# Attention beside an MLP: who copies the scores and the sums out of PSUM, and in which order

## The chip, the cores and the metric

The kernel runs on one core of a Trainium2 chip. The metric is the device time of one execution in microseconds (us), as the median of several runs. The core has five engines that run side by side and wait for each other by semaphores: TensorE (PE; its weight loads are PEld), VectorE (DVE), ScalarE (ACT), GpSimd (POOL) and SyncE (SP), which here issues the transfers (DMA). TensorE writes only to PSUM, which has eight banks of 128 x 512 fp32 elements. VectorE and ScalarE read PSUM; GpSimd does not.

## The reference

Shapes: x is 1 x 2048 x 448; 16 query heads of 28 columns share one key head and one value head; the MLP is 1792 wide. All is fp32.

```python
def _A_ref(x, wq, wk, wv, wo):
    q = (x @ wq).reshape(B, S, 16, 28).transpose(0, 2, 1, 3)
    k = x @ wk
    v = x @ wv
    p = softmax(einsum("bhqd,bkd->bhqk", q, k) * 28 ** -0.5)
    o = einsum("bhqk,bkd->bhqd", p, v)
    return o.transpose(0, 2, 1, 3).reshape(B, S, 448) @ wo

def _B_ref(x, w1, w2):
    return maximum(x @ w1, 0) @ w2

xn = layernorm(x)
return x + _A_ref(xn, wq, wk, wv, wo) + _B_ref(xn, w1, w2)
```

## The kernel before

The program has two parts. The first, up to about 338 us, normalizes and transposes x, makes queries, keys and values (kept in a scratch in DRAM) and runs the MLP into the accumulator `acc`. The second is the attention, and the change is there.

The attention runs over 16 units `u`, each of 512 queries (a block `b`) and four heads (a group `g`); `b` is the outer loop. A unit has 2048 keys, which are 16 key blocks `kb` of 128. It runs in two halves of 8 key blocks. A half has two stages, one after the other on TensorE:

- The score stage: 32 score matmuls (8 key blocks x 4 heads), each 128 keys x 512 queries into one PSUM bank (line 588). A string of letters in `HALVES` gives their order. For an "a", the bank is of the pool `psA` (four banks), and ScalarE reads it and writes the exponential to the tile `p` in SBUF (line 605). For a "d", the bank is of `psD` (three banks), and VectorE copies the raw score to `p` (line 610); ScalarE makes the exponential later, from SBUF in place, four heads at a time (line 623). "a" fills the key blocks from 0 up, "d" those from `KA` = 5 up, so that 20 scores go the first way and 12 the second.
- The PV run: for each key block, the four heads' matmuls of `p` with the values (line 477, `pv`). They are listed as eight matmul instructions a block. They add up in one bank over the unit's 16 key blocks; `vtile` has columns of ones, so that the softmax sums come out as further rows. We call what is in this bank the sums. Before, it is a pool of its own, `psO`, of one bank.

The first half's run leaves its last block (`behind`), which goes first in the second half's run; the second half's run thus has nine blocks and ends the unit. In the first half's run, at place `MPOS`, stand the maxima of the next unit (`maxima`, line 370): a few score matmuls into a "d" bank, a transpose and a reduction on VectorE, and eight small DMAs that put the negated estimates in two further rows of the next unit's query stack `qst`. The score matmul then subtracts them (114 rows: four times 28 and these two).

When a unit's last block is done, ScalarE copies the sums to `oS` (line 480), and four DMAs spread the denominators (`dens`). Later, at the letter "R" in the next unit's first half, `recips` takes the reciprocals on VectorE, writes them to DRAM and reads them back spread over the partitions (`rb`), and `normalized` multiplies and splits on GpSimd (`on`, `oH`, `oL`). The four output projections of that unit (`o_proj`, line 522: three matmuls of 448 columns into a "d" bank, added to `acc` by VectorE, line 524) come at the letters "F", two in each half, from the second half on. The very last half makes two at each "F". `finish` handles the sums of the last unit by itself.

Each engine works in the order of the program. A score matmul thus waits until the bank that it is to write has been read by the engine that had it, four "a" or three "d" uses earlier; an output projection is one of the "d" uses. `load_stack` loads the query stack of the unit after the next, between a first half's score stage and its run. The tiles `p` have ten buffers.

Of the kernel before, what the change touches and what calls it, by code (L numbers as in the profile page):

```python
# [8 lines left out]
F32 = mybir.dt.float32  # L9
# [29 lines left out]
def program(ctx: ExitStack, tc: tile.TileContext, HM, fine, x, wq, wk, wv, wo, w1, w2, out):  # L39
    nc = tc.nc  # L40
# [21 lines left out]
    WARM = 28  # L62
    KQ = 4 * DH
    NU = NQB * NHG
    NA, ND, NST = 4, 3, 3
    assert DR == 64 and KQ + 2 <= P and HG * 32 == P and NPART * FP == DFF

    cst = ctx.enter_context(tc.tile_pool(name="cst", bufs=1))
    small = ctx.enter_context(tc.tile_pool(name="small", bufs=2))
    dram = ctx.enter_context(tc.tile_pool(name="dram", bufs=1, space=DRAM))  # L70
    psA = ctx.enter_context(tc.tile_pool(name="psA", bufs=NA, space=PSUM))
    psD = ctx.enter_context(tc.tile_pool(name="psD", bufs=ND, space=PSUM))
    psO = ctx.enter_context(tc.tile_pool(name="psO", bufs=1, space=PSUM))


    acc = cst.tile([P, NT, D], F32, name="acc")
# [15 lines left out]
    gone = cst.tile([P, TPB + 3], F32, name="gone")  # L92
    nc.vector.memset(gone, 1.0)

    pw = psD.tile([P, QB], F32, name="d")
    for _ in range(WARM):
        nc.tensor.matmul(pw[:, 0:P], ident, ident, start=True, stop=True)  # L97
    kst = cst.tile([P, S], F32R, name="kst")
# [137 lines left out]
    def transposed(b, xn, chunks=range(DC + 1)):  # L236
        xs = slice(b * QB, (b + 1) * QB)
        for c in chunks:
            pt = psD.tile([P, QB], F32, name="d") if c < DC else psO.tile([P, QB], F32, name="o")
            for i in range(TPB):  # L240
                nc.tensor.transpose(pt[:, i * P : (i + 1) * P], xn[i][:, c * P : (c + 1) * P], ident)  # L241
            if c < DC:
                nc.scalar.activation(xH[:, c, xs], pt, AF.Copy)  # L243
                nc.vector.tensor_tensor(xL[:, c, xs], pt, xH[:, c, xs].bitcast(F32), op=ALU.subtract)  # L244
            else:
                tmp = small.tile([P, QB], F32R, name="tmp")
                nc.scalar.activation(xR[0:DR, xs], pt[0:DR], AF.Copy)
                nc.scalar.activation(tmp[DR:P], pt[DR:P], AF.Copy)
                nc.vector.tensor_tensor(xR[DR:P, xs], pt[DR:P], tmp[DR:P].bitcast(F32), op=ALU.subtract)  # L249
# [86 lines left out]

    def v_rows():

        pv = psD.tile([P, QB], F32, name="d")
        for kb in range(NKB):  # L340
            nc.tensor.transpose(pv[:, kb * 32 : kb * 32 + DH], vT[0][:, kb * P : (kb + 1) * P], ident[0:DH, 0:DH])
        nc.vector.tensor_copy(vtile[:, :, 0:DH], pv.rearrange("p (i d) -> p i d", d=32)[:, :, 0:DH])
        if fine is not None:
            nc.vector.tensor_reduce(
                gone[:, TPB : TPB + 1], vtile[:, :, 0:DH], axis=AX.XY, op=ALU.max, apply_absolute_value=True
            )
# [15 lines left out]
    def maxima(u):  # L362

        st = qst[u]

        def scores(kb):
            pm = psD.tile([P, QB], F32, name="d")
            for j in range(HG):
                c = slice(32 * j, 32 * j + 32)
                nc.tensor.matmul(  # L370
                    pm[c], kstF[0:KQ, kb * 32 : kb * 32 + 32], st.bitcast(F32)[0:KQ, j], start=True, stop=True
                )
            return pm

        n = QB // 32
        nm = small.tile([P, n], F32, name="nm")
        nm2 = small.tile([P, 2, n], F32R, name="nm2")
        rows = small.tile([P, 2 * n], F32, name="rows")
        sc = scores(0)
        if HM > 1:  # L380
            top = small.tile([P, QB], F32R, name="tmp").bitcast(F32)
            nc.vector.tensor_copy(top, sc)
            for kb in range(1, HM):
                nc.vector.tensor_tensor(top, top, scores(kb), op=ALU.max)
            sc = top
        mt = small.tile([P, QB], F32R, name="tmp").bitcast(F32)
        nc.vector.transpose(mt, sc)
        nc.vector.tensor_reduce(nm, mt.rearrange("p (c k) -> p c k", k=32), axis=AX.X, op=ALU.max, negate=True)
        nc.vector.tensor_copy(nm2[:, 0], nm)
        nc.vector.tensor_tensor(nm2[:, 1], nm, nm2[:, 0].bitcast(F32), op=ALU.subtract)  # L390
        nc.vector.transpose(rows, nm2.rearrange("p s n -> p (s n)").bitcast(F32))
        for j in range(HG):
            for s in range(2):
                r = KQ + s
                nc.sync.dma_start(
                    st.bitcast(F32)[r : r + 1, j].rearrange("o (c q) -> o c q", q=32),
                    rows[32 * j + s * n : 32 * j + s * n + n],
                )
# [17 lines left out]
    def mlp_down(p, b, i, between=None):  # L416
        hH, hL = hid[p, b]
        wd = parts[p][1]
        py = psO.tile([P, QB], F32, name="o") if i == 1 else psA.tile([P, QB], F32, name="a")
        n = 0  # L420
        for f in range(FC):
            for hm, wi in ((hH, 0), (hH, 1), (hL, 0)):
                nc.tensor.matmul(  # L423
                    py[:, 0:D], hm[:, f, i * P : (i + 1) * P], wd[:, wi, f, :], start=n == 0, stop=n == 3 * FC - 1
                )
                n += 1
            if between:
                between()
        t = b * TPB + i
        nc.vector.tensor_tensor(acc[:, t, :], py[:, 0:D], acc[:, t, :], op=ALU.add)  # L430
# [41 lines left out]
    def pv(u, kb, p):  # L472
        start, stop = kb == 0, kb == NKB - 1
        if start:
            o_acc[u] = psO.tile([P, QB], F32, name="o")
        for j in range(HG):
            nc.tensor.matmul(o_acc[u][32 * j : 32 * j + 32], vtile[:, kb, :], p[:, j], start=start, stop=stop)  # L477
        if stop and u < NU - 1:
            oS = opool.tile([P, QB], F32, name="oS")
            nc.scalar.activation(oS, o_acc.pop(u), AF.Copy)  # L480
            o_sb[u] = oS
            dens(u)

# [31 lines left out]
    def o_proj(u, i):  # L515

        b, g = units[u]
        oH, oL = o_hl[u]
        py = psD.tile([P, QB], F32, name="d")[:, 0:D]
        c = slice(i * P, (i + 1) * P)  # L520
        for n, (om, wm) in enumerate(((oH, woH), (oH, woL), (oL, woH))):
            nc.tensor.matmul(py, om[:, c], wm[:, g, :], start=n == 0, stop=n == 2)  # L522
        t = b * TPB + i
        nc.vector.tensor_tensor(acc[:, t, :], py, acc[:, t, :], op=ALU.add)  # L524
        if g == NHG - 1:
            nc.sync.dma_start(out[t * P : (t + 1) * P, :], acc[:, t, :])

    def finish(u):

        b, g = units[u]  # L530
        o = o_acc.pop(u)
        if fine is not None:
            nc.vector.tensor_reduce(gone[:, TPB + 1 : TPB + 2], dsum, axis=AX.X, op=ALU.add)
            nc.vector.scalar_tensor_tensor(
# [16 lines left out]
                nc.vector.tensor_reduce(gone[:, i : i + 1], dens, axis=AX.XY, op=ALU.add)  # L551
            nc.gpsimd.tensor_scalar(rb[:, i], r[:, i].to_broadcast([P, HG, 32]), 1.0, 0.0, op0=ALU.mult, op1=ALU.add)
        for i, c in enumerate(cols):
            pb = psD.tile([P, QB], F32, name="d")
            nc.tensor.transpose(pb[:, 0:P], rb[:, i].rearrange("p j c -> p (j c)"), ident)
            nc.vector.tensor_tensor(on[:, c], pb[:, 0:P], oS[:, c], op=ALU.mult)
        if fine is not None:
# [8 lines left out]
            nc.vector.tensor_tensor(acc[:, t, :], py[:, 0:D], acc[:, t, :], op=ALU.add)  # L566
            nc.sync.dma_start(out[t * P : (t + 1) * P, :], acc[:, t, :])
        if fine is not None:
            pg = psD.tile([P, QB], F32, name="d")
            nc.tensor.matmul(pg[0:1, 0:1], gone[:, TPB : TPB + 1], gone[:, TPB + 2 : TPB + 3], start=True, stop=True)  # L570
            nc.vector.tensor_scalar(fine, pg[0:1, 0:1], 1e20, None, op0=ALU.is_le)

# [6 lines left out]

    HALVES = "adaadaadFaaaddadaaaFadaadadaRdadada", "adaadaadddaaadaFaadaadFaadadaadada"
    KA, KH, MPOS = 5, NKB // 2, 3
    todo = []

    def score(u, kb, j, p, pt):
        nc.tensor.matmul(  # L588
# [1 line left out]
        )  # L590
        return p[:, j]

    for u in range(NU):
        for half, order in enumerate(HALVES):
            ps, n_a, n_d = {}, 0, KA * HG
            for k in order:
                if k in "ad":
                    n = n_a if k == "a" else n_d
                    kb, j = n // HG, n % HG
                    if j == 0:  # L600
                        ps[kb] = ppool.tile([P, HG, QB], F32, name="p")
                if k == "a":
                    pt = psA.tile([P, QB], F32, name="a")
# [1 line left out]
                    nc.scalar.activation(p, pt, AF.Exp, scale=SCALE)  # L605
                    n_a += 1
                elif k == "d":
                    pt = psD.tile([P, QB], F32, name="d")
                    p = score(u, half * KH + kb, j, ps[kb], pt)
                    nc.vector.tensor_copy(p, pt)  # L610
                    n_d += 1
                elif k == "R" and u:
                    recips(u - 1)
                    normalized(u - 1)
                    todo += [(u - 1, i) for i in range(TPB)]
                elif k == "F":
                    for _ in range(2 if half and u == NU - 1 else 1):
                        if todo:
                            o_proj(*todo.pop(0))
            if half == 0 and u:  # L620
                load_stack(u + NST - 1)
            for kb in range(KA, KH):
                nc.scalar.activation(ps[kb], ps[kb], AF.Exp, scale=SCALE)  # L623
            run = [(half * KH + kb, ps[kb]) for kb in range(KH)]
            if half:
                run.insert(0, behind)
            else:
                behind = run.pop()
            for n, (kb, p) in enumerate(run):
                if half == 0 and n == MPOS and u < NU - 1:  # L630
                    maxima(u + 1)
                pv(u, kb, p)
    assert not todo
    finish(NU - 1)


# [23 lines left out]
```

## Time and profile before

| | us |
|---|---|
| median of 3 runs | 883.08 (882.75 to 883.5) |
| the profiled execution | 882.62 |
| its span, from the first to the last instruction | 880.8 |
| TensorE busy | 871.0 (99%) |
| ScalarE busy | 562.2 (64%) |
| VectorE busy | 471.0 (53%) |
| attention, from the first score to the end of the span | 338.1 to 880.8 |

Busy shares are over the whole span; in the attention they are different, and are shown below by stage. A profile line has the source line, the engine, the operation, the tile written and the tiles read, the shape and a count; then either start and length, or total busy time, mean length in ns and idle time. A matmul's length includes its way through the array, and matmuls overlap, so that only the distance between two starts says what one costs.

### The profile page before, as it was taken

To read this page: it belongs to the slowest core of one execution; us is meant where nothing else is said; L and a number is where in the kernel's file an instruction comes from. 1 tells how busy PE (TensorE), PEld (TensorE's weight loads), DVE (VectorE), ACT (ScalarE), POOL (GpSimd) and SP (SyncE) were. 2 spreads that over 40 slices of the span, in tenths; PEclk is the share of its full clock that TensorE was granted. 3 is DMA by queue.
4 is the path that set the end of the run, shared out by engine and by line. 5 is a ranking of instruction groups with operands and counts; after the bars stand their busy time and mean duration, and the time that the engine had idled before them with its cause. 6 is when DMAs were issued, how large, how long until landed. Compare 5 with 4: busy or idle time off the path is not lost.

```text
span 880.8 us, 12946 instructions
## 1 busy us (share of the span) xinstructions
PE 871.0 (99%) x4998; PEld 573.0 (65%) x4998; DVE 471.0 (53%) x848; ACT 562.2 (64%) x871; POOL 113.3 (13%) x96
## 2 busy tenths in 40 slices
PE   9999999999999999999999999999999999999996
PEld 8788888888888886454554554554554554554562
DVE  6833344333333346474574574574574574574563
ACT  4541111111111116999999999999999999999993
POOL 3034202020202003010110110110110110110110
PEclk9999999999999999999999999999999999999998
DMA  6868050010000001020120230120230120230001
GB/s 214 293 200 167 4 132 23 23 45 1 1 1 1 0 2 38 2 56 25 33 56 21 57 77 21 36 56 20 58 77 15 42 56 17 62 77 14 2 13 46
DMA packets 37502, 45.89 MB, mean 52 GB/s; under 512 B 13640, under 2 KB 24072, under 8 KB 37264
## 3 DMA queue, kind: packets, MB, share of 16 engines
q1 hardware_dynamic: 37432, 44.98, 19.7%
q8 instruction: 41, 0.67, 0.3%
q14 instruction: 29, 0.24, 0.1%
HBM read 32.37 MB, written 12.18 MB: 51 GB/s over the span
## 4 chain that ended last, share of the span: by engine, by line
PE 98%; DVE 1%; ACT 1%; issue 0%; POOL 0%; POOLq 0%
PE o L477 25%; PE a L588 19%; PE a L187 16%; PE a L423 12%; PE d L588 10%; PE d L522 4%; PE o L423 4%; PE a L192 4%; PE d L370 2%; PE a L271 1%; PE d L97 1%; PE d L241 1%; ACT p L623 0%; PE a L565 0%; DVE qs L255 0%
## 5 line engine op out<-in xcount | busy, mean ns | idle before, releaser
L610 DVE COPY p<-d 128x512 f32<-128x512 f32 x384 | 246.1, 686 | 161.7 <-PE d L588 142.1
L605 ACT ACTIVATE p<-a 128x512 f32<-128x512 f32 x640 | 317.1, 708 | 21.7 <-PE a L588 21.7
L477 PE MATMUL o<-p,vtile 128*32 128x512 f32 x2048 | 229.5, 594 | 0.0
L588 PE MATMUL a<-qst,kst 114*128 114x512 f32 x640 | 225.4, 407 | 0.0
L410 ACT ACTIVATE hH<-a 128x512 fp32r<-128x512 f32 x56 | 33.5, 598 | 235.9 <-PE a L192 235.9
L623 ACT ACTIVATE p<-p 128x2048 f32<-128x2048 f32 x96 | 183.1, 2131 | 0.0
L588 PEld LDWEIGHTS a<-qst,kst 114*128 114x128 f32 x640 | 120.0, 187 | 77.2 <-ACT p L605 28.1
L477 PEld LDWEIGHTS o<-p,vtile 128*32 128x32 f32 x2048 | 61.6, 109 | 144.1 <-issue 128.3
L588 PE MATMUL d<-qst,kst 114*128 114x512 f32 x384 | 145.8, 400 | 0.0
L187 PE MATMUL a<-xH,w 128*128 128x512 f32 x408 | 104.8, 392 | 0.2 <-ACT xH L243 0.2
L411 DVE SCALAR_TENSOR_TENSOR hL<-a,hH 128x512 fp32r<-128x512 f32 x56 | 38.7, 692 | 118.4 <-ACT hH L410 118.4
L423 PE MATMUL a<-w,hH 128*128 128x448 f32 x336 | 95.6, 366 | 0.0
L187 PEld LDWEIGHTS a<-xH,w 128*128 128x128 f32 x408 | 76.1, 188 | 16.5 <-ACT xH L243 0.8
L588 PEld LDWEIGHTS d<-qst,kst 114*128 114x128 f32 x384 | 72.4, 188 | 12.9 <-DVE p L610 4.5
L508 POOL TENSOR_TENSOR on<-rb,oS 128x512 f32<-128x512 f32 x15 | 19.4, 1290 | 448.4 <-DMA rb<-rscr 418.0
L430 DVE TENSOR_TENSOR acc<-a,acc 128x448 f32<-128x448 f32 x84 | 52.2, 622 | 33.7 <-PE a L423 33.7
L423 PEld LDWEIGHTS a<-w,hH 128*128 128x128 f32 x336 | 63.0, 188 | 6.3
L423 PE MATMUL a<-w,hL 128*128 128x448 f32 x168 | 61.2, 364 | 0.0
L187 PE MATMUL a<-xL,w 128*128 128x512 f32 x204 | 57.7, 390 | 0.1
L187 PEld LDWEIGHTS a<-xL,w 128*128 128x128 f32 x204 | 38.3, 188 | 8.8 <-DVE xL L244 0.7
L192 PE MATMUL a<-xR,w 128*128 128x512 f32 x136 | 42.0, 390 | 0.2 <-DVE xR L249 0.2
L524 DVE TENSOR_TENSOR acc<-d,acc 128x448 f32<-128x448 f32 x60 | 37.3, 622 | 5.3 <-PE d L522 5.3
(111 smaller groups left out, 577.4 us busy)
## 6 DMA issues: line engine op xcount, KB each, us to landing
qst<-qscr SPq DMA_DIRECT2D x64, 224.0 KB
qscr<-qs SPq DMA_DIRECT2D x16, 512.0 KB
rb<-rscr SPq DMA_DIRECT2D x60, 64.0 KB
acc<-in_A_x SPq DMA_DIRECT2D x16, 224.0 KB
out<-acc SPq DMA_DIRECT2D x16, 224.0 KB
stg<-in_B_w SPq DMA_DIRECT2D x7, 448.0 KB
stg<-in_B_w SPq DMA_DIRECT2D x7, 384.0 KB
qst<-rows SPq DMA_DIRECT2D x128, 2.0 KB
```

Source lines behind the costliest of these rows:

```text
L187: nc.tensor.matmul(ps, lhs[:, wi, c, cols], xm[:, c, xs], start=n == 0, stop=False)
L192: nc.tensor.matmul(ps, lhs[:, wi, DC, cols], xR[:, xs], start=False, stop=wi == 1)
L411: nc.vector.scalar_tensor_tensor(hL[:, f], ph, 0.0, hH[:, f].bitcast(F32), op0=ALU.max, op1=ALU.subtract)
L423: nc.tensor.matmul(py[:, 0:D], hm[:, f, i * P : (i + 1) * P], wd[:, wi, f, :], start=n == 0, stop=n == 3 * FC - 1)
L430: nc.vector.tensor_tensor(acc[:, t, :], py[:, 0:D], acc[:, t, :], op=ALU.add)
L477: nc.tensor.matmul(o_acc[u][32 * j : 32 * j + 32], vtile[:, kb, :], p[:, j], start=start, stop=stop)
L522: nc.tensor.matmul(py, om[:, c], wm[:, g, :], start=n == 0, stop=n == 2)
L524: nc.vector.tensor_tensor(acc[:, t, :], py, acc[:, t, :], op=ALU.add)
L588: nc.tensor.matmul(pt, kst[0 : KQ + 2, kb * P : (kb + 1) * P], qst[u][0 : KQ + 2, j, :], start=True, stop=True)
L605: nc.scalar.activation(p, pt, AF.Exp, scale=SCALE)
L610: nc.vector.tensor_copy(p, pt)
L623: nc.scalar.activation(ps[kb], ps[kb], AF.Exp, scale=SCALE)
```

## The change

- VectorE, not ScalarE, copies the sums out of PSUM.
- A half has 19 "a" scores and 13 "d" scores (`HA` = 19). Key block 4 of a half is mixed: three heads by ScalarE, one by VectorE, with an exponential of one head later.
- `psD` now has four banks, named d0 to d3 and handed out in a ring by `d_tile`; `psO` is gone. The bank with the sums is taken out of the ring (`keep`) and comes back when the sums have been copied. The few other users of `psO` use the ring.
- Every PV run leaves its last block to the next run, over the border of units too, except at the end of the last two units. A unit's block 15 is thus the first block of the next unit's first run.
- "R" moves to near the end of the second half (`ends` does it for the units that have ended); in the last unit it stands after each half's score stage. The projections of a unit start one half later, and the last half makes three at each "F".
- The maxima move from the fourth to the second place of the first half's run.
- Both strings in `HALVES` are new.

```diff
-    NA, ND, NST = 4, 3, 3
+    NA, ND, NST = 4, 4, 3
...
-    psD = ctx.enter_context(tc.tile_pool(name="psD", bufs=ND, space=PSUM))
-    psO = ctx.enter_context(tc.tile_pool(name="psO", bufs=1, space=PSUM))
+    psD = ctx.enter_context(tc.tile_pool(name="psD", bufs=1, space=PSUM))
+    ring = [f"d{i}" for i in range(ND)]
+
+    def d_tile(keep=False):
+        name = ring.pop(0)
+        if not keep:
+            ring.append(name)
+        t = psD.tile([P, QB], F32, name=name)
+        return (t, name) if keep else t
...
     def pv(u, kb, p):
         start, stop = kb == 0, kb == NKB - 1
         if start:
-            o_acc[u] = psO.tile([P, QB], F32, name="o")
+            o_acc[u] = d_tile(keep=True)
+        o = o_acc[u][0]
         for j in range(HG):
-            nc.tensor.matmul(o_acc[u][32 * j : 32 * j + 32], vtile[:, kb, :], p[:, j], start=start, stop=stop)
+            nc.tensor.matmul(o[32 * j : 32 * j + 32], vtile[:, kb, :], p[:, j], start=start, stop=stop)
         if stop and u < NU - 1:
             oS = opool.tile([P, QB], F32, name="oS")
-            nc.scalar.activation(oS, o_acc.pop(u), AF.Copy)
+            nc.vector.tensor_copy(oS, o)
+            ring.append(o_acc.pop(u)[1])
             o_sb[u] = oS
             dens(u)
...
-    HALVES = "adaadaadFaaaddadaaaFadaadadaRdadada", "adaadaadddaaadaFaadaadFaadaadadaada"
-    KA, KH, MPOS = 5, NKB // 2, 3
-    todo = []
+    HALVES = "adadadaadaadadaFaaddadaaFadaaddaad", "adadadaadaaddaadaFadaadadaFadaaRdad"
+    HA, KH = 19, NKB // 2
+    todo, behind, ended = [], [], []
...
+    def ends():
+        for u in ended:
+            recips(u)
+            normalized(u)
+            todo.extend((u, i) for i in range(TPB))
+        ended.clear()
...
     for u in range(NU):
+        last = u == NU - 1
         for half, order in enumerate(HALVES):
-            ps, n_a, n_d = {}, 0, KA * HG
+            ps, n_a, n_d = {}, 0, HA
...
-                elif k == "R" and u:
-                    recips(u - 1)
-                    normalized(u - 1)
-                    todo += [(u - 1, i) for i in range(TPB)]
-                elif k == "F":
-                    for _ in range(2 if half and u == NU - 1 else 1):
+                elif k == "R":
+                    ends()
+                else:
+                    for _ in range(3 if last and half else 1):
                         if todo:
                             o_proj(*todo.pop(0))
+            if last:
+                ends()
             if half == 0 and u:
                 load_stack(u + NST - 1)
-            for kb in range(KA, KH):
-                nc.scalar.activation(ps[kb], ps[kb], AF.Exp, scale=SCALE)
-            run = [(half * KH + kb, ps[kb]) for kb in range(KH)]
-            if half:
-                run.insert(0, behind)
-            else:
-                behind = run.pop()
-            for n, (kb, p) in enumerate(run):
-                if half == 0 and n == MPOS and u < NU - 1:
+            for kb in range(HA // HG, KH):
+                h = slice(max(HA - kb * HG, 0), HG)
+                nc.scalar.activation(ps[kb][:, h], ps[kb][:, h], AF.Exp, scale=SCALE)
+            run = behind + [(u, half * KH + kb, ps[kb]) for kb in range(KH)]
+            behind = [] if half and u >= NU - 2 else [run.pop()]
+            for n, (v, kb, p) in enumerate(run):
+                if half == 0 and n == 1 and not last:
                     maxima(u + 1)
-                pv(u, kb, p)
-    assert not todo
+                pv(v, kb, p)
+                if kb == NKB - 1 and not (last and half):
+                    ended.append(v)
+    assert not todo and not behind
     finish(NU - 1)
```

More of the change, by code (lines that the diff above doesn't have):

```diff
@@ L93, in program @@
     nc.vector.memset(gone, 1.0)
-    pw = psD.tile([P, QB], F32, name="d")
+    pw = d_tile()
     for _ in range(WARM):
@@ L238, in transposed @@
         for c in chunks:
-            pt = psD.tile([P, QB], F32, name="d") if c < DC else psO.tile([P, QB], F32, name="o")
+            pt = d_tile()
             for i in range(TPB):
@@ L337, in v_rows @@
     def v_rows():
-        pv = psD.tile([P, QB], F32, name="d")
+        pv = d_tile()
         for kb in range(NKB):
@@ L366, in scores @@
         def scores(kb):
-            pm = psD.tile([P, QB], F32, name="d")
+            pm = d_tile()
             for j in range(HG):
@@ L418, in mlp_down @@
         wd = parts[p][1]
-        py = psO.tile([P, QB], F32, name="o") if i == 1 else psA.tile([P, QB], F32, name="a")
+        py = d_tile() if i == 1 else psA.tile([P, QB], F32, name="a")
         n = 0
@@ L518, in o_proj @@
         oH, oL = o_hl[u]
-        py = psD.tile([P, QB], F32, name="d")[:, 0:D]
+        py = d_tile()[:, 0:D]
         c = slice(i * P, (i + 1) * P)
@@ L530, in finish @@
         b, g = units[u]
-        o = o_acc.pop(u)
+        o = o_acc.pop(u)[0]
         if fine is not None:
@@ L553, in finish @@
         for i, c in enumerate(cols):
-            pb = psD.tile([P, QB], F32, name="d")
+            pb = d_tile()
             nc.tensor.transpose(pb[:, 0:P], rb[:, i].rearrange("p j c -> p (j c)"), ident)
@@ L568, in finish @@
         if fine is not None:
-            pg = psD.tile([P, QB], F32, name="d")
+            pg = d_tile()
             nc.tensor.matmul(pg[0:1, 0:1], gone[:, TPB : TPB + 1], gone[:, TPB + 2 : TPB + 3], start=True, stop=True)
             nc.vector.tensor_scalar(fine, pg[0:1, 0:1], 1e20, None, op0=ALU.is_le)
-    HALVES = "adaadaadFaaaddadaaaFadaadadaRdadada", "adaadaadddaaadaFaadaadFaadadaadada"
-    KA, KH, MPOS = 5, NKB // 2, 3
-    todo = []
+    HALVES = "adadaadadaadadaFaaddadaaFadaaddaad", "adadadaadaaddaadaFadaadadaFaadaRdad"
+    HA, KH = 19, NKB // 2
+    todo, behind, ended = [], [], []
     def score(u, kb, j, p, pt):
@@ L599, in program @@
                     kb, j = n // HG, n % HG
-                    if j == 0:
+                    if kb not in ps:
                         ps[kb] = ppool.tile([P, HG, QB], F32, name="p")
@@ L607, in program @@
                 elif k == "d":
-                    pt = psD.tile([P, QB], F32, name="d")
+                    pt = d_tile()
                     p = score(u, half * KH + kb, j, ps[kb], pt)
```

## The prediction

> **What bounds the kernel now.** I read the page's busy shares and chain first, to see which engine to follow, then busy time by stage, then the timeline of TensorE, ScalarE and VectorE over one attention unit.
>
> ```profile
> PE 871.0 (99%) x4998; PEld 573.0 (65%) x4998; DVE 471.0 (53%) x848; ACT 562.2 (64%) x871; POOL 113.3 (13%) x96
> ...
> PE 98%; DVE 1%; ACT 1%; issue 0%; POOL 0%; POOLq 0%
> ```
>
> Both point at TensorE, but a matmul that waits for a PSUM bank also counts as busy. So the question is how far apart the matmuls start. The stages, in the view of busy time by stretch (length first, then each engine):
>
> ```profile
> 338.12:347.04 8.92, 8.92 (x34) 5.33 (x32) 7.23 (x12) 8.43 (x18) 2.44 (x2) 1.00 0.41 92
> 354.04:363.02 8.98, 8.98 (x36) 5.39 (x32) 7.19 (x12) 8.44 (x18) 0.00 (x0) 1.00 0.03 4
> 370.91:380.04 9.13, 9.13 (x36) 5.38 (x32) 6.71 (x13) 8.92 (x19) 0.00 (x0) 1.00 0.01 1
> ...
> 602.59:611.77 9.18, 9.18 (x43) 6.76 (x39) 7.65 (x15) 8.92 (x19) 0.00 (x0) 1.00 0.01 1
> 611.77:618.78 7.01, 7.01 (x66) 1.97 (x65) 3.20 (x8) 6.84 (x7) 0.70 (x1) 1.00 0.53 129
> 618.78:627.80 9.02, 9.02 (x42) 6.76 (x38) 7.97 (x13) 8.43 (x18) 2.51 (x3) 1.00 0.32 86
> 627.80:635.69 7.89, 7.89 (x73) 2.14 (x73) 0.78 (x2) 6.84 (x7) 0.00 (x0) 1.00 0.00 0
> ...
> 849.70:859.92 10.22, 10.22 (x49) 8.08 (x45) 9.15 (x15) 9.39 (x19) 1.44 (x2) 1.00 0.01 2
> 403.96:834.36 430.40, 430.40 (x2761) 229.66 (x2757) 259.87 (x455) 403.43 (x611) 41.80 (x39) 1.00 0.18 42
> ```
>
> The last row is 13 units: 33.11 us each. One unit is two score stages (9.18 and 9.02) and two PV runs (7.01: seven key blocks and the maxima; 7.89: nine blocks). The first three rows are the halves without output projections, 849.70 the last half, with four. The granted clock is 1.00 throughout. Now TensorE inside one unit:
>
> ```profile
> 606.79 1.12 PE L588 MATMUL a<-qst,kst 114*128 114x512 f32 x3
> 607.75 0.36 PE L522 MATMUL d<-woH,oH 128*128 128x448 f32 x1
> ...
> 608.36 0.40 PE L588 MATMUL a<-qst,kst 114*128 114x512 f32 x1
> ...
> 609.31 0.40 PE L588 MATMUL d<-qst,kst 114*128 114x512 f32 x1
> ...
> 610.93 0.42 PE L588 MATMUL a<-qst,kst 114*128 114x512 f32 x1
> ...
> 618.78 0.50 PE L588 MATMUL a<-qst,kst 114*128 114x512 f32 x1
> 619.11 0.39 PE L588 MATMUL d<-qst,kst 114*128 114x512 f32 x1
> ...
> 620.51 0.98 PE L588 MATMUL d<-qst,kst 114*128 114x512 f32 x3
> 621.32 0.85 PE L588 MATMUL a<-qst,kst 114*128 114x512 f32 x3
> ...
> 627.46 0.42 PE L588 MATMUL a<-qst,kst 114*128 114x512 f32 x1
> 627.80 7.96 PE L477 MATMUL o<-p,vtile 128*32 128x512 f32 x72
> ```
>
> From 609.31 to 610.93 lie seven scores: 0.231 each (0.232 below, with the small slips). One output projection of three matmuls takes 608.36 - 607.75 = 0.61. The first score of a stage takes 0.33, thus 0.10 extra, and the step into the PV run 0.34, 0.11 extra. A half without a wait is then 32 x 0.232 + 2 x 0.61 + 0.21 = 8.85. It takes 9.18 and 9.02, and the rows show where: three scores from 606.79 take 0.96, not 0.70 (0.26 lost); three from 620.51 take 0.81 (0.11 lost). Without these both halves are 8.91 to 8.92. The PV runs have nothing to give: 0.877 a block in 7.89, without a gap.
>
> The other two engines:
>
> ```profile
> 602.85 0.60 ACT L480 ACTIVATE oS<-o 128x512 f32<-128x512 f32 x1 [1.31 <-issue]
> 603.34 9.90 ACT L605 ACTIVATE p<-a 128x512 f32<-128x512 f32 x20
> 612.87 5.74 ACT L623 ACTIVATE p<-p 128x2048 f32<-128x2048 f32 x3
> 619.37 9.91 ACT L605 ACTIVATE p<-a 128x512 f32<-128x512 f32 x20 [0.76 <-PE a L588]
> 628.92 5.72 ACT L623 ACTIVATE p<-p 128x2048 f32<-128x2048 f32 x3
> 619.61 3.81 DVE L610 COPY p<-d 128x512 f32<-128x512 f32 x6 [2.03 <-PE d L588]
> 626.09 2.48 DVE L610 COPY p<-d 128x512 f32<-128x512 f32 x4
> L605 ACT ACTIVATE p<-a 128x512 f32<-128x512 f32 x640 | 317.1, 708 | 21.7 <-PE a L588 21.7
> L610 DVE COPY p<-d 128x512 f32<-128x512 f32 x384 | 246.1, 686 | 161.7 <-PE d L588 142.1
> ```
>
> ScalarE starts an exponential every (628.92 - 619.37) / 20 = 0.4775 us, each 0.71 long, the first 0.59 after the stage begins (619.37 - 618.78), and in a unit's first half 0.75 after, since the copy of the sums is in front. A copy train on VectorE has a step of (2.48 - 0.69) / 3 = 0.60, the first 0.83 after the stage begins. With four "a" banks the 12th "a" score of the first half must wait for the 8th exponential: 603.34 + 7 x 0.4775 + 0.71 = 607.39, while TensorE could start it at 606.79 + 2 x 0.232 = 607.25. That is the 0.26 (0.14 of wait, some 0.02 of release, 0.10 restart). In the second half it is the third of three "d" scores in a row on three banks. So TensorE is the limit, and bank waits worth 0.37 us of 33.11 in a unit are all that a reordering can return.
>
> The Trainium skill, "Perfetto Trace Analysis", Identifying the Most-Contended Engine, says that matmul busy share is a poor measure, and that weight-load share should be compared with the other engines' occupancy. By that rule ScalarE would be the bound here; it returns below as a rival.
>
> **The change, part by part.**
>
> *One "a" fewer, one "d" more in each half.* TensorE still issues 32 scores: nothing. ScalarE drops 0.4775 and gains one exponential of a single head from SBUF: at least a quarter of L623's step, (5.74 / 3) / 4 = 0.48, at most a lone 0.60. So between 0 and +0.12, I take +0.04; it lies in the 0.76 us for which ScalarE waits at the boundary and costs nothing. Without that cover it would be 32 x 0.04 = 1.3 us. VectorE gains one step, 0.60.
>
> *The new order.* I follow the banks with the figures above, from the stage's start: a score every 0.232, a projection 0.61. In the first half the tightest place is the 9th "a", wanted at 3.35 and free at 0.59 + 4 x 0.4775 + 0.71 + 0.03 = 3.24. In the second half the 10th "a" is wanted at 3.82, free at 3.72; the first projection (8th user of a "d" bank) wanted at 4.05, free at 0.83 + 4 x 0.60 + 0.69 + 0.03 = 3.95; the second projection (12th user, with 0.05 more for the add of the first) wanted at 6.51, free at 6.40. Everywhere there is 0.10 us or more. The same working on the old orders finds the wait of the first half, and for that of the second a margin of 0.04 where the trace has a wait, so it is good to about 0.05. No wait should be left, which gives 8.85 by steps, or 8.92 by the old halves less their seen waits; I take 8.89.
>
> *The copy of the sums moves from ScalarE to VectorE.* ScalarE loses 0.60 in 15 units; it then starts a unit's first half 0.59 after TensorE, as in the second. VectorE pays 0.69 (L610's form). It waits for the previous unit's block 15, now the first block of the run. Behind it on VectorE stand only the maxima's transposes, which wait for TensorE anyway: 2.47 us idle in front of them (row below). Behind it on SP's queue stand the four loads of the sums and the maxima's row transfers, due half a unit later. Bounds: 0 (covered) to 15 x 0.69 = 10.4 if it delayed the ring; I take 0, since the next "d" score comes some 6 us later.
>
> *Every run leaves one block.* The number of blocks and of switches is the same, so two runs of 7.01 and 7.89 become 7.87 and 7.01. The last block's exponential now has half a stage to end. The old 9-block run waited hardly at all for it (0.877 a block), so the gain is 0 to 0.03 a unit; I take 0.
>
> *Maxima at the second place, one ring of four.* Same matmuls, about 1.7 us earlier; while sums accumulate, three banks are left for scores, as before. The next sums take a bank whose copy has ended; nothing. In the MLP stage the same four banks serve the transposes and one down projection: nothing.
>
> *Reciprocals and projections move by about half a unit.*
>
> ```profile
> 610.94 0.24 DVE L497 RECIPROCAL r<-d 128x16 f32<-128x16 f32 x1
> ...
> 615.48 0.72 DVE L387 STREAM_TRANSPOSE tmp<-d 128x512 f32<-128x512 f32 x1 [2.47 <-PE d L370]
> 618.08 1.29 POOL L508 TENSOR_TENSOR on<-rb,oS 128x512 f32<-128x512 f32 x1 [31.31 <-DMA rb<-rscr]
> ...
> 620.16 1.30 POOL L512 TENSOR_TENSOR oL<-on,oH 128x512 fp32r<-128x512 f32 x1
> ```
>
> From reciprocal to oL are 621.46 - 610.94 = 10.5 us, by way of one DMA out and four back on SP's queue, here with a stack load (4 x 224 KB) issued right behind. The new place is three scores before the end of a second half, about 9.0 after its start; oL is then ready 19.5 after it, 3.6 into the next half (15.9 later). The first projection wants oL at 3.58 + 0.41 = 4.0. That holds by 0.4, and the stack load no longer stands behind it. If it failed, each 0.1 would cost 13 x 0.1 = 1.3 us and a restart of 0.10.
>
> One more half runs without projections (four, not three) and the last half has six, not four. Halves without projections are held by ScalarE: 8.92, 8.98, 9.13, mean 9.01, with 20 steps of 0.4775. With 19 they lie between 9.01 - 0.48 = 8.53 and 9.01; each wait costs a restart, so 8.75. The last half: 8.89 + 4 x 0.61 = 11.33.
>
> **Sum.** Before: 27.03 (three halves) + 14 x 9.18 + 14 x 9.02 + 10.22 = 292.1. After: 4 x 8.75 + 27 x 8.89 + 11.33 = 286.4. That is 5.7 less. The profiled execution took 882.62, its span 880.8 and 1.8 around it; 882.6 - 5.7 = 876.9. The median of the runs is 883.08, 0.46 above it, so 877.4.
>
> **Rivals.**
>
> *The margins are too thin: same.* A wait of any size cost 0.11 at 620.51. One left in each half gives back 27 x 0.11 = 3.0 (880.4), two give 6 (883.4). For it: margins of 0.10 against an error of 0.05. Against: that the waits of the old orders came where the working puts them.
>
> *VectorE becomes the bound: slower.* L610's busy time is 246.1 / 384 = 0.64 a copy. If 0.66 were the step in the new stages, the last "d" (15th user) could start only at 0.83 + 11 x 0.66 + 0.10 + 0.69 + 0.03 = 8.91, not 8.52; the half would be 9.28, and 27 halves 0.18 above their old mean of 9.10: 4.9, plus some 1 for the half without projections, 889. It decides from a step of about 0.64. Against it stands the 0.60 in the row of four.
>
> *ScalarE is the bound after all: much faster.* Over the 13 units it is busy 403.43 / 430.40 = 94%, weight loads 53%. By the Trainium skill's rule (the same page and section) it is the most contended engine; the evenly spaced starts of TensorE do not bear that out. If it were the bound, its copy (603.34 - 602.85 = 0.49) and the wait of 1.31 before it would leave each of 15 units: 27 us, 856. Against: ScalarE is the one with waits, 0.76 and 1.31.
>
> **How the numbers follow.** Forecast 0.67 (its own range 875 to 879.5), thin margins 0.17 (880 to 884.5), VectorE 0.12 (885 to 891), ScalarE 0.04. No change is what a measurement cannot tell, within 0.2%: 881.3 to 884.8. Thin margins fall mostly into it: faster 0.74, same 0.14, slower 0.12. The range 874.5 to 885 leaves out the last two cases.
>
> **What would show it.** Both score stages at 8.85 to 8.95, with no slow triple of scores; PV runs of 7.87 and 7.01; ScalarE's idle at both boundaries without the copy of sums; VectorE's copy of sums ending before the transposes; POOL's oL ended before each half's first projection. Wrong if "d" scores start late behind VectorE copies, or if the unit stays at 33.1.

## The result

The changed kernel takes 877.36 us (876.87 to 878.03, six runs) against 883.1 (882.75 to 883.5): a ratio of 0.9936, 95% interval 0.9923 to 0.9948. That is 5.7 us faster, 0.65%, clear of the noise. The profiled execution took 876.87, its span 875.0. A later set of five runs gave 877.25.

The page of the changed kernel, busy shares:

```profile
PE 865.4 (99%) x4998; PEld 579.8 (66%) x4998; DVE 487.0 (56%) x895; ACT 555.6 (63%) x856; POOL 113.3 (13%) x96
```

They tell as little as before: TensorE is busy for 99%, and five microseconds less. The stages tell more. Busy time by stretch, changed kernel (length, then PE, PEld, DVE, ACT, POOL; the first two rows are the first and the last of the four halves without projections, then one unit's two score stages and two runs, the last half, and eleven units in one row):

```profile
338.70:347.36 8.66, 8.66 (x34) 5.52 (x32) 7.66 (x13) 8.17 (x18) 2.08 (x2) 1.00 0.43 95
...
386.72:395.49 8.77, 8.77 (x36) 5.37 (x32) 7.04 (x14) 8.18 (x18) 0.00 (x0) 1.00 0.01 1
...
598.33:607.16 8.83, 8.83 (x43) 7.02 (x39) 7.94 (x14) 8.24 (x19) 1.95 (x3) 1.00 0.32 68
607.16:615.02 7.86, 7.86 (x73) 2.22 (x72) 3.73 (x8) 7.06 (x7) 0.00 (x0) 1.00 0.03 4
615.02:623.90 8.88, 8.88 (x43) 6.90 (x39) 7.97 (x16) 8.28 (x18) 0.00 (x0) 1.00 0.01 1
623.90:630.90 7.00, 7.00 (x65) 1.97 (x65) 1.25 (x4) 7.00 (x7) 1.60 (x2) 1.00 0.12 39
842.91:854.31 11.40, 11.40 (x55) 8.98 (x51) 10.44 (x18) 9.48 (x19) 3.08 (x3) 1.00 0.01 3
435.14:794.07 358.93, 358.93 (x2337) 199.12 (x2333) 230.11 (x418) 336.38 (x507) 33.72 (x33) 1.00 0.19 45
```

A unit takes 358.93 / 11 = 32.63, not 33.11. Both score stages are at 8.8 to 8.9, where they were 9.18 and 9.02; the two runs add up to 14.86, as before (14.90). So the time came out of the score stages, as it had to.

TensorE, around the 10th "a" and the first projection of a second half, two of the places that the prediction called tightest (start and length of each stretch):

```profile
617.69 0.63 PE L598 MATMUL d<-qst,kst 114*128 114x512 f32 x2
618.16 0.63 PE L598 MATMUL a<-qst,kst 114*128 114x512 f32 x2
618.62 0.40 PE L598 MATMUL d<-qst,kst 114*128 114x512 f32 x1
618.86 0.40 PE L598 MATMUL a<-qst,kst 114*128 114x512 f32 x1
619.10 0.37 PE L533 MATMUL d<-woH,oH 128*128 128x448 f32 x1
```

From 617.69 to 619.10 there are six scores in 1.41, 0.235 each: the 9th and 10th "a" and the first projection all start without a wait. The engines that empty the banks, same kernel:

```profile
598.93 9.41 ACT L624 ACTIVATE p<-a 128x512 f32<-128x512 f32 x19 [0.59 <-PE a L598]
...
615.62 9.42 ACT L624 ACTIVATE p<-a 128x512 f32<-128x512 f32 x19 [1.40 <-PE a L598]
...
608.36 0.69 DVE L490 COPY oS<-d 128x512 f32<-128x512 f32 x1
609.15 0.72 DVE L396 STREAM_TRANSPOSE tmp<-d 128x512 f32<-128x512 f32 x1
...
615.86 4.28 DVE L629 COPY p<-d 128x512 f32<-128x512 f32 x7 [4.61 <-PE d L598]
...
631.31 1.30 POOL L523 TENSOR_TENSOR oL<-on,oH 128x512 fp32r<-128x512 f32 x1
```

ScalarE now idles 0.59 and 1.40 at the two borders of a unit; VectorE's copies still start every (4.28 - 0.69) / 6 = 0.60, and its copy of the sums ends before the transposes; oL is ready 632.61 - 630.90 = 1.7 after the stage begins.

Two second halves are an exception, at 9.1. The same two come again in the second profiled execution (9.15 and 9.09), so they are not the chance of one execution. In the later one, VectorE's first seven copies took 4.49 in place of 4.28. In the earlier one ScalarE began late, for a reason that the trace does not show:

```profile
517.08:526.19 9.11, 9.11 (x42) 6.68 (x38) 8.18 (x16) 8.24 (x18) 0.00 (x0) 1.00 0.09 29
...
517.95 9.41 ACT L624 ACTIVATE p<-a 128x512 f32<-128x512 f32 x19 [1.72 <-PE d L598]
```

It starts 0.87 after the stage, not 0.60, and this delay of 0.27 costs the half 0.24: the margins are small.

### The profile page after: what moved, and what is told of

The parts are those of the page before. It is cut to its first block, busy times and chain, and to the rows that moved or that the text cites. A ratio compares the mean times of both kernels' runs of the same rounds, so it can differ in the third digit from the quotient of the medians.

```text
span 875.0 us, 13029 instructions
## 1 busy us (share of the span) xinstructions
PE 865.4 (99%) x4998; PEld 579.8 (66%) x4998; DVE 487.0 (56%) x895; ACT 555.6 (63%) x856; POOL 113.3 (13%) x96
## 4 chain that ended last, share of the span: by engine, by line
PE 98%; DVE 1%; ACT 0%; issue 0%; POOL 0%; POOLq 0%
PE d L487 25%; PE a L598 17%; PE a L196 16%; PE a L432 12%; PE d L598 11%; PE d L533 4%; PE d L432 4%; PE a L201 4%; PE d L379 2%; PE d L106 1%; PE a L280 1%; PE d L250 1%; PE a L576 0%; DVE qs L264 0%; ACT p L643 0%
## 5 line engine op out<-in xcount | busy, mean ns | idle before, releaser
L629 DVE COPY p<-d 128x512 f32<-128x512 f32 x416 | 258.8, 681 | 170.0 <-PE d L598 162.0
L624 ACT ACTIVATE p<-a 128x512 f32<-128x512 f32 x608 | 301.5, 691 | 41.8 <-PE a L598 40.1
L487 PE MATMUL d<-p,vtile 128*32 128x512 f32 x2048 | 229.4, 594 | 0.0
L598 PE MATMUL a<-qst,kst 114*128 114x512 f32 x608 | 218.0, 404 | 0.0
L643 ACT ACTIVATE p<-p 128x2048 f32<-128x2048 f32 (+1 forms) x128 | 198.2, 1771 | 0.0
L487 PEld LDWEIGHTS d<-p,vtile 128*32 128x32 f32 x2048 | 62.9, 109 | 146.5 <-issue 135.3
L598 PE MATMUL d<-qst,kst 114*128 114x512 f32 x416 | 156.5, 395 | 0.0
L598 PEld LDWEIGHTS a<-qst,kst 114*128 114x128 f32 x608 | 114.0, 187 | 63.5 <-issue 23.5
L598 PEld LDWEIGHTS d<-qst,kst 114*128 114x128 f32 x416 | 78.3, 188 | 13.8 <-DVE p L629 2.1
```

Source lines behind the costliest of these rows:

```text
L487: nc.tensor.matmul(o[32 * j : 32 * j + 32], vtile[:, kb, :], p[:, j], start=start, stop=stop)
L598: nc.tensor.matmul(pt, kst[0 : KQ + 2, kb * P : (kb + 1) * P], qst[u][0 : KQ + 2, j, :], start=True, stop=True)
L643: nc.scalar.activation(ps[kb][:, h], ps[kb][:, h], AF.Exp, scale=SCALE)
```

## The experiments

The theory: TensorE is the bound, and the only time to win is in waits for PSUM banks in the score stages, which the new orders and the split of 19 and 13 return. The rivals: it is the copy taken off ScalarE; it is the block that every run leaves; it is ScalarE's total work. The strings of the two kernels, letter for letter, are these (in the diff of the section on the change, some letters stand otherwise):

```python
HALVES = "adaadaadFaaaddadaaaFadaadadaRdadada", "adaadaadddaaadaFaadaadFaadadaadada"  # before
HALVES = "adadaadadaadadaFaaddadaaFadaaddaad", "adadadaadaaddaadaFadaadadaFaadaRdad"  # changed
```

**Only the new orders**, on the kernel before.

```diff
-    HALVES = "adaadaadFaaaddadaaaFadaadadaRdadada", "adaadaadddaaadaFaadaadFaadadaadada"
-    KA, KH, MPOS = 5, NKB // 2, 3
+    HALVES = "adadaadadaadadaFaaddadaaFadaaddRaad", "adadadaadaaddaadaFadaadadaFaadadad"
+    HA, KH, MPOS = 19, NKB // 2, 3
...
```

> The kernel before with nothing but the new strings and the split of 19 and 13 (R stays in the first half, ahead of its last three scores); ScalarE still copies the sums, only first halves leave a block, psO stays. Theory (the gain is bank waits in the score stages, returned by order and split): first halves 9.0 (ScalarE starts 0.16 later than in the changed kernel, so the 7th a score waits 0.03 and costs a restart), second halves 8.87, three halves without projections 8.7; sum 5.5 less than before, 877.6 us. Rival (the gain comes from taking the copy off ScalarE, or from the block that every run leaves): 881 or more.

Measured: 880.25 us, ratio 0.997 (0.9959 to 0.9981). That is between the two, 2.65 above the theory's figure. A first half, a second half, the nine-block run behind it, and ScalarE's last exponentials in that run:

```profile
601.38:610.37 8.99, 8.99 (x43) 6.79 (x39) 8.07 (x14) 8.73 (x19) 0.00 (x0) 1.00 0.01 1
617.37:626.31 8.94, 8.94 (x43) 6.93 (x39) 8.02 (x14) 8.38 (x19) 2.65 (x3) 1.00 0.41 88
626.31:634.31 8.00, 8.00 (x73) 2.13 (x72) 1.07 (x2) 6.95 (x7) 0.00 (x0) 1.00 0.08 29
...
627.07 6.20 ACT L624 ACTIVATE p<-p 128x512 f32<-128x512 f32 x4
```

First halves are as the theory had them. Second halves are 0.07 above it, and the run takes 8.00 in place of 7.89: with a shorter score stage in front, its ninth block comes before the exponential that it needs. That ends at 627.07 + 6.20 = 633.27, and the ninth block starts at 633.32, 0.98 after the eighth, where a block otherwise takes 0.86. Both excesses together are 14 x 0.18 = 2.5, nearly the whole miss. I had not counted it.

**Only the copy on VectorE**, on the kernel before.

```diff
-            nc.scalar.activation(oS, o_acc.pop(u), AF.Copy)
+            nc.vector.tensor_copy(oS, o_acc.pop(u))
```

> The kernel before with nothing but the copy of the sums on VectorE. Theory: ScalarE starts a unit's first half 0.16 earlier, which is just what the 12th a score of that half waits for; VectorE starts its first copy some 0.07 later. First halves 8.92 to 9.07 in place of 9.18, second halves stay at 9.02: 1.5 to 3.6 less, 879.5 to 881.6 us. Rival (the copy on ScalarE is what bounds the unit): the whole gain or more, 877 or less. Rival (the copy was hidden): 883.

Measured: 880.47 us, ratio 0.9972 (0.9963 to 0.9982).

```profile
601.37:610.38 9.01, 9.01 (x42) 6.80 (x38) 8.19 (x16) 8.42 (x18) 0.00 (x0) 1.00 0.01 2
617.39:626.41 9.02, 9.02 (x42) 6.75 (x38) 7.98 (x13) 8.42 (x18) 2.05 (x3) 1.00 0.31 85
```

First halves fall from 9.18 to 9.01, second ones stay. One line brings half of the gain, not by freeing ScalarE's time but because its first exponential comes 0.16 earlier in that half, which was the wait of the 12th "a" there. Of the 0.26 lost at that place 0.12 stays: the three scores from 605.56 still take 0.82, not 0.70.

**The copy back on ScalarE**, on the changed kernel.

```diff
-            nc.vector.tensor_copy(oS, o)
+            nc.scalar.activation(oS, o, AF.Copy)
```

> The changed kernel with the copy of the sums back on ScalarE, at its new place, thus behind the four exponentials of the first half. Theory (TensorE is the bound, ScalarE has over 0.7 us to spare at that border): no change, 877.4 within 0.6. Rival (ScalarE is the bound): 15 x 0.49 = 7.4 more, 884.7 us.

Measured: 876.81 us, ratio to the kernel before 0.9932 (0.9918 to 0.9945), the same as the changed kernel within the intervals. The timeline of ScalarE:

```profile
411.96 6.20 ACT L643 ACTIVATE p<-p 128x512 f32<-128x512 f32 x4
417.88 0.77 ACT L490 ACTIVATE oS<-d 128x512 f32<-128x512 f32 x1
419.62 2.56 ACT L624 ACTIVATE p<-a 128x512 f32<-128x512 f32 x5 [0.96 <-PE a L598]
```

A copy on the same engine costs nothing here, since 0.96 us of idle time still follow it. So the rival that ScalarE's total work is the bound falls. Taken with the run before: what matters is what stands behind the copy, not who makes it. That ScalarE can still set the pace inside a score stage is shown by two runs below.

**The old orders and the old split**, on the changed kernel.

```diff
-    HALVES = "adadaadadaadadaFaaddadaaFadaaddaad", "adadadaadaaddaadaFadaadadaFaadaRdad"
-    HA, KH = 19, NKB // 2
+    HALVES = "adaadaadFaaaddadaaaFadaadadadadada", "adaadaadddaaadaFaadaadFaadadaadRada"
+    HA, KH = 20, NKB // 2
```

> The changed kernel with the old strings and the old split of 20 and 12 (R in the second half, ahead of its last three scores); the copy on VectorE, the block left by every run and the ring stay. Theory: first halves 8.95 to 9.07, second halves 9.03 with the old wait at three d scores in a row, four halves without projections at 9.05: 881 to 883.5 us. Rival (the structure makes the gain): 877 to 879.

Measured: 884.05 us, ratio 1.0012 (1.0003 to 1.0021). The whole gain is gone and a little more, and the run is 0.55 above the expected range. A regular first half, and one of the exceptions:

```profile
667.97:677.00 9.03, 9.03 (x42) 6.83 (x39) 7.66 (x13) 8.43 (x18) 1.63 (x2) 1.00 0.28 56
799.82:809.64 9.82, 9.26 (x43) 6.80 (x39) 7.73 (x13) 8.54 (x18) 2.86 (x3) 1.00 0.00 1
```

In the exceptions, six first halves, the first projection, which these orders put at the ninth place, waits for oL on GpSimd. Against 9.02 they lose 2.3 us together; without them the run would lie in the range. With reciprocals at the end of a second half, the projection must come later, as the new orders have it.

**No block left over the border of units**, on the changed kernel.

```diff
-            behind = [] if half and u >= NU - 2 else [run.pop()]
+            behind = [] if half else [run.pop()]
```

> The changed kernel, but second halves' runs leave no block, so a unit ends in its own nine-block run as before. Theory: nine blocks last until ScalarE has just ended the last exponential, so block 15 waits 0 to 0.2 in each unit, and VectorE's copy of the sums stands in front of the next half's first copy by 0.1; 0 to 4 us more than the changed kernel, 877.4 to 881. Rival (the block left over is worth most of the gain): 882 to 883.

Measured: 879.96 us, ratio 0.9962 (0.9948 to 0.9975), thus 2.6 more than the changed kernel. The nine-block run and the score stage behind it:

```profile
724.38:732.43 8.05, 8.05 (x74) 2.14 (x73) 1.25 (x4) 7.00 (x7) 2.93 (x3) 1.00 0.12 34
732.43:741.28 8.85, 8.85 (x42) 7.02 (x38) 8.55 (x15) 8.26 (x18) 0.25 (x1) 1.00 0.41 91
```

The score stages keep their 8.85; the run takes 0.16 more than 7.89, which is 2.2 for 14 of them. So the block left over does earn something, though only once the score stages are short.

**One letter in each half: 20 and 12.** The last "d" of each string becomes an "a", on the changed kernel.

```diff
-    HALVES = "adadaadadaadadaFaaddadaaFadaaddaad", "adadadaadaaddaadaFadaadadaFaadaRdad"
-    HA, KH = 19, NKB // 2
+    HALVES = "adadaadadaadadaFaaddadaaFadaaddaaa", "adadadaadaaddaadaFadaadadaFaadaRdaa"
+    HA, KH = 20, NKB // 2
```

> The changed kernel with one letter changed in each string: the last d is an a, so the split is 20 and 12 again. Theory: ScalarE is late for the last a scores, which wait for the exponential four before; each half 9.04, those without projections 9.0: 27 x 0.17 + 1.2 = 5.8 more, 883 us. Rival (the order matters and the split does not): 877 to 879.

Measured: 881.41 us, ratio 0.9979 (0.997 to 0.9988): 4.1 more than the changed kernel. A first half; the second half of the unit takes 9.03 too:

```profile
715.63:724.66 9.03, 9.03 (x43) 6.88 (x39) 8.12 (x16) 8.43 (x18) 0.00 (x0) 1.00 0.01 1
```

Both are as the theory said, and 27 x 0.16 is 4.3. The 1.2 that I had put on the halves without projections is there too: they take 8.91, 8.97, 9.02 and 9.02, 1.0 more in sum than the changed kernel's. It doesn't show in the time of the profiled execution (880.28, the lowest of the eleven), whose attention began at 337.73, 1.0 earlier than the changed kernel's; why, the record does not say.

**One letter the other way: 18 and 14.**

```diff
-    HALVES = "adadaadadaadadaFaaddadaaFadaaddaad", "adadadaadaaddaadaFadaadadaFaadaRdad"
-    HA, KH = 19, NKB // 2
+    HALVES = "adadaadadaadaddFaaddadaaFadaaddaad", "adadadaadaaddaadaFadaadadaFaadaRddd"
+    HA, KH = 18, NKB // 2
```

> The changed kernel with one letter changed the other way in each string: one a is a d, 18 and 14. Theory: VectorE, with 14 copies and two adds in a stage, is late for the last d scores, halves 9.3, while halves without projections gain 0.4: 27 x 0.45 - 1.6 = 10.5 more, 888 us. Rival (VectorE has time to spare, and only ScalarE limits): 877 or less.

Measured: 889.48 us, ratio 1.0071 (1.0058 to 1.0085), 12.1 more than the changed kernel. A first and a second half, the place of the wait in the first, and that in the second:

```profile
435.91:445.33 9.42, 9.23 (x42) 7.00 (x39) 8.58 (x15) 8.26 (x17) 1.29 (x1) 1.00 0.20 50
453.20:462.49 9.29, 9.14 (x42) 6.85 (x38) 8.32 (x16) 8.70 (x19) 0.00 (x0) 1.00 0.01 1
...
439.05 0.74 PE L598 MATMUL d<-qst,kst 114*128 114x512 f32 x2
439.98 0.44 PE L533 MATMUL d<-woH,oH 128*128 128x448 f32 x1 [0.19 <-DVE p L629]
...
461.27 0.63 PE L598 MATMUL d<-qst,kst 114*128 114x512 f32 x2
462.06 0.50 PE L598 MATMUL d<-qst,kst 114*128 114x512 f32 x1 [0.15 <-DVE p L629]
```

Two "d" scores that should take 0.46 take 0.93, and the projection behind them waits for VectorE. In the second half the last of three "d" in a row starts 0.33 late. That is what the working gives for VectorE's load: the 16th user of a "d" bank finds it free at 0.83 + 12 x 0.60 + 0.10 + 0.69 + 0.03 = 8.85 and wants it at 8.51. So the theory holds for second halves. In first halves the wait comes at another place than I had expected, in the middle, where the new letter puts two "d" and a projection in a row on three banks; nothing waits behind it, and the half takes 0.13 more. So the order counts beside the load. Without projections, too, the same split takes 8.17 and 8.27 in first halves and 9.07 and 9.14 in second ones. The rival of the prediction in which VectorE is the bound lies one letter away. By the working no order would save 18 and 14 here, but none other was tried with projections.

**ScalarE half a microsecond late**, on the changed kernel: one more copy at the head of each stage.

```diff
+    late = opool.tile([P, QB], F32, name="late", bufs=1)
...
+                    if n_a == 0:
+                        nc.scalar.activation(late, pt, AF.Copy)
                     nc.scalar.activation(p, pt, AF.Exp, scale=SCALE)
```

> The changed kernel with one more ScalarE operation at the head of each score stage: a copy of the first a bank (128 x 512) to a tile that nobody reads, ahead of its exponential. It makes ScalarE 0.48 late within the stage, of the 0.9 us for which it is idle at each border. Theory (four a banks, margins of 0.1): the 7th or 9th a score waits about 0.36 and costs a restart of 0.10, the half takes 9.3 in place of 8.86, those without projections 0.48 more: 27 x 0.45 + 4 x 0.48 + 0.5 = 14.6 more, 892 us. Rival (what counts is ScalarE's idle time in a half): hidden, 877.4.

Measured: 891.11 us, ratio 1.0092 (1.0077 to 1.0108), 13.8 more.

```profile
404.18:413.50 9.32, 9.32 (x42) 6.70 (x38) 8.17 (x14) 8.84 (x20) 2.11 (x3) 1.00 0.24 51
...
405.91 0.50 PE L599 MATMUL a<-qst,kst 114*128 114x512 f32 x1
406.24 0.39 PE L599 MATMUL d<-qst,kst 114*128 114x512 f32 x1
406.47 0.92 PE L599 MATMUL a<-qst,kst 114*128 114x512 f32 x2
407.22 0.40 PE L599 MATMUL d<-qst,kst 114*128 114x512 f32 x1
...
421.96 0.60 ACT L626 ACTIVATE late<-a 128x512 f32<-128x512 f32 x1 [1.41 <-PE a L599]
```

The same kind of operation that was free behind the exponentials costs about 0.45 a half at the head, although ScalarE has 1.41 us of idle time right in front of it. It cannot use that time, since it reads the first bank that the stage fills; so the idle time at a border does not help inside the stage. With four banks TensorE follows ScalarE's lateness almost at once: the fifth "a", at 405.91, is the first whose next step is long (0.33), and the two "a" from 406.47 take 0.75, not 0.46.

**An order for the halves without projections.** There VectorE has the time of two adds to spare, so 18 "a" and 14 "d", in an order of their own, in the first two units.

```diff
+    FREE = "adaddaaaddaadadaadadadaadadadada", "adaddaaaddaadadaadadadaadadadRada"
...
-        for half, order in enumerate(HALVES):
+        HA = 18 if u < 2 else 19
+        for half, order in enumerate(FREE if u < 2 else HALVES):
```

> The changed kernel with an order of its own, 18 a and 14 d spread evenly, in the four halves of the first two units, which have no projections. Theory: there VectorE has the time of two adds to spare and ScalarE limits; the four halves take 8.2 each in place of 8.66 to 8.78: 2.1 less, 875.3 us. Rival (something else holds these halves): no change, 877.4.

Measured: 877.23 us, ratio 0.993 (0.9916 to 0.9943): nothing gained in the time. Its four halves did take 8.07 to 8.23, but in that execution the attention began later and the program ended later, so I ran it once more, beside the changed kernel (877.25).

> The kernel with its own order in the first two units, once more. Its four halves were 2.1 us shorter in sum, but start and end of that execution were 0.8 and 1.3 us longer than the changed kernel's. If these belong to the execution: 875.3 to 876.3. If they belong to the program: 877.2 as before.

Measured: 876.99 us, ratio 0.9931 (0.9917 to 0.9944). Its first half without projections, and the end of the program from the first transpose of `finish` on, here and in the changed kernel:

```profile
338.77:346.84 8.07, 8.07 (x33) 5.29 (x31) 7.87 (x14) 7.55 (x16) 1.60 (x1) 1.00 0.46 102
...
861.05:874.53 13.48, 5.12 (x18) 2.56 (x18) 4.62 (x19) 0.46 (x3) 1.09 (x4) 0.79 0.22 75
```

```profile
862.77:875.04 12.27, 5.12 (x18) 2.55 (x18) 4.62 (x19) 0.45 (x3) 1.09 (x4) 0.83 0.24 83
```

The late start was one execution's; the late end came again. The busy times in it are the same, so 1.2 us go where no engine works. (The last half was longer too, 11.58 and 11.59 in the two executions, not 11.30 or 11.40; I did not follow that.) The last drains of VectorE, as instructions of the closing line (times of the first and the last), with the own order and in the changed kernel:

```profile
L677 DVEq DRAIN  x2: 17/72/128, 871.5 to 874.2; - x2
L677 DVEq EVENT_SEMAPHORE  x2: 21/21/21, 872.8 to 874.5; - x2
```

```profile
L675 DVEq DRAIN  x2: 10/14/17, 873.2 to 874.6; - x2
L675 DVEq EVENT_SEMAPHORE  x2: 21/21/21, 874.5 to 875.0; - x2
```

With the own order, VectorE's last drain comes 1.4 us after the semaphore before it, not 0.1, and holds up the end. What it waited for the trace does not name. A fetch of instructions would fit: VectorE's program had become longer (899 instructions in the page, not 895), and in the stretch 872.8:874.2, between that semaphore and that drain, the view of transfers lists one of the kind instruction, of 16 KB, and no other (queue, packets, MB, share of the 16 transfer engines; in the changed kernel the last such transfer starts behind the drain):

```profile
q8 instruction: 1, 0.02, 4.6%
```

There is a way to try it.

**Both: the own order, and the copy of the sums on ScalarE**, so that VectorE's program is shorter again.

> The own order of the first two units, and the copy of the sums on ScalarE at its new place, so that VectorE's program is 15 copies shorter again. The two executions with the own order ended 1.2 us later than the changed kernel because VectorE reached its last instruction late, behind a fetch of instructions. If the length of VectorE's program does that: the end is back at 12.3 us after the last score stage's work, 875.2 to 876.2. If not: 877, as with the own order alone.

Measured: 875.17 us (874.62 to 875.33), ratio 0.9913 (0.99 to 0.9927), the fastest of all: 2.1 under the changed kernel. The end is back:

```profile
860.49:872.82 12.33, 5.12 (x18) 2.55 (x18) 4.53 (x19) 0.46 (x3) 1.08 (x4) 0.87 0.24 83
L677 DVEq DRAIN  x2: 10/14/17, 871.0 to 872.4; - x2
```

That taking copies out of VectorE's program brought the end back is shown by this pair only. It is not the length as such: with 18 and 14 in every half VectorE has 927 instructions, and its last drain, at 887.3, comes 0.1 after the semaphore at 887.2, as in the changed kernel. What decides between 895, 899 and 927 no run shows; that it is a fetch stays a guess.

## Why the prediction was right

- *TensorE is the bound, and bank waits are all there is to win.* Right. The copy back on ScalarE changes nothing in the new place, and the forecast of 877.4 fell 0.04 from the median, closer than its own error deserves. Part of that is luck: summed over the traces, the 32 score stages fell from 292.2 to 286.0 us, 6.2 and not 5.7, while the attention began 0.6 later (338.70, not 338.12).
- *No wait is left; 8.89 a half.* Right: 8.83 and 8.88 in the unit shown. The working by banks also held at the other orders: 9.04 for 20 and 12 (9.03 measured), 9.3 for a late ScalarE (9.32), 9.3 for 18 and 14 (9.29 and 9.42, in first halves at another place than I had said).
- *Halves without projections 8.75.* They took 8.66 to 8.77. *The last half 11.33.* It took 11.40.
- *The lone exponential costs nothing.* ScalarE idles 0.59 and 1.40 at the borders, so it is covered.
- *The copy of the sums: nothing on VectorE, 0.16 earlier on ScalarE.* Right in the sum. At its old place it is worth 2.75 us by itself; at the new one, in the middle of a run, either engine can make it.
- *The block left over: 0 to 0.03 a unit.* Right against the kernel before, wrong as a part. I read its worth from the old run, which hardly waited. Without it, the shorter score stages would have lost 2.6 us, nearly all of it to the last block's exponential. It is not a gain of its own but keeps one.
- *Reciprocals to oL in 10.5, a margin of 0.4.* Right as the slowest case. In the unit shown it is 632.61 - 623.69 = 8.9, with 2.3 to spare. But over the 15 units of the two profiled executions the step takes 8.5 to 10.8, and in the slowest unit, in the second execution, oL ended 798.54 - 798.17 = 0.37 before its projection:

```profile
796.88 1.29 POOL L523 TENSOR_TENSOR oL<-on,oH 128x512 fp32r<-128x512 f32 x1
...
798.54 0.36 PE L533 MATMUL d<-woH,oL 128*128 128x448 f32 x1
```

With the old orders, which want oL 1.6 earlier, the wait did come.

The three rivals: thin margins (they showed in two halves of 32), VectorE as the bound (it needed a step of 0.64, and the step stayed at 0.60; with one letter more it is, 889.48), ScalarE as the bound (its total work is not: a copy more in each of 15 units cost nothing; its pace inside a stage is, as soon as it starts late). The Trainium skill, "Perfetto Trace Analysis", Identifying the Most-Contended Engine, names the engine with the highest occupancy as the one to optimize; for TensorE it leaves the matmul share out and goes by the weight-load share and by the share of the peak rate that the matmuls reach. By occupancy that would be ScalarE here, and the run with the copy on it shows that its busy time does not set the time. The share of the peak rate was not worked out in this case. The Trainium skill's warning against the matmul share is fair all the same: 99% was true before and after.

## What to carry to other kernels

Where a profile shows the matmul engine full, read the distance between starts of matmuls: steps that repeat are work, and a step that is too long is a wait with a restart behind it. Then work out, from the step of each engine that empties the banks, when each bank is free and when it is wanted; this gave most stages here to within 0.15 us, and missed where something outside the banks was late, as oL with the old orders. Parts of a change don't simply add up. The orders alone brought 3.0 us and the copy alone 2.75, which happen to make the 5.7 of the whole; but everything without the orders lost 0.8, and everything without the block left over brought 3.3, since a shorter stage makes the next one wait for what used to be in time.

## What was not expected of the hardware

- A ScalarE copy of a 128 x 512 bank costs nothing behind the exponentials, and about 0.45 a half at the head of a stage, with 1.41 us of idle time in front of it.
- A score that has waited is mostly followed by a step of 0.33 to 0.34 in place of 0.23, thus by about 0.10 more (406.24 - 405.91 above); the first score of a stage too. Some steps of 0.25 to 0.29 stand alone, so it is not so for every small delay.
- The end of the program took 13.5 us in place of 12.3, with the same work in it, in both executions with four instructions more on VectorE, and 12.3 again with fifteen fewer than that. A kernel with still more of them did not have it.
